# Attention with a relative position bias, then a mixture of adapters: a planner that knows of a shared port, bias multiplies over two chunks, and a reordered opening

## The chip, the core and the metric

The kernel runs on one core of one Trainium2 chip. Its time is the device time of one execution, in microseconds. Before the change it is 222.62 us, the median of 3 runs (222.09 to 223.76). One further execution was taken by the hardware profiler; all rows of a profile shown here come from such single executions.

In the profile PE is the TensorE matmul, PEld its weight load, DVE is VectorE, ACT is ScalarE, POOL is GpSimd and SP is SyncE; a "q" behind a name (SPq, ACTq) is the engine's queue issuing a DMA. L65 is the line of a helper through which all VectorE and GpSimd instructions pass, so these are told apart by the names of what they write and read.

## The reference, cut to what matters

Two stages follow each other. The first is attention over 8 batches, 8 heads, 576 positions and 64 columns a head, with a bias that depends on the distance of two positions alone:

```python
scores = scale * np.matmul(q, k.transpose(0, 1, 3, 2))
n = np.abs(pos[:, None] - pos[None, :])
bucket = np.where(n < half, n, np.minimum(large, n_buckets - 1))
scores = scores + bias_table[bucket].transpose(2, 0, 1)[None]
attn = softmax(scores); x = attn @ v
```

All distances from 128 on share one bucket. Since softmax does not change when one number is taken off a whole row, the bias can be taken relative to that last bucket; it then differs from zero only in a band around the diagonal.

The second stage treats the 4608 rows of x (512 columns). Eight gates are computed by `x @ w_gate`, the two largest are kept and turned into weights, and each chosen adapter adds `weight * (x @ A[e]) @ B[e]` to x, with A and B of rank 16.

## The kernel before

The unit of work is a *pair*: two heads of one batch. There are 32 pairs, four to a batch, taken in order. Of the 576 positions, 512 form the main part (four key chunks of 128 keys, each against 512 queries and both heads) and 64 form the tail. Pair i passes through these steps:

- SyncE issues the loads: k in two transfers (L164), q in one (L170), v in two (L164); once a batch the tails of k and q (L176, four transfers) and of v (L182, two).
- GpSimd casts k, q and v to bfloat16 (kb, qb, vn), and once a batch the tails (tl, vt).
- PE transposes kb and qb into a PSUM tile (kqps, L264), and VectorE copies it to SBUF (kqT).
- PE computes the scores: chunks 0 to 3 are the main part (L281), each a PSUM tile of 128 x 1024. Chunk 4 (L286 to L294) holds the tail keys and the tail queries; there the bias is added by matmuls against MT and MH. ScalarE takes the exp of each chunk (L301, p<-sc), five a pair. One small exp a batch (ptt) covers tail against tail.
- VectorE multiplies the band of chunks 0 to 3 by the exp of the bias (`band`, L304; p<-p,M), one instruction a chunk. A middle chunk has 768 elements a partition, an outer one 512.
- PE multiplies with v (L324 to L333, pv), VectorE takes the reciprocal of the sums (rc) and scales (x<-pv,rc).

After the fourth pair of a batch follows the *mixture* of that batch (L631), interleaved with the next batch's pairs: transposes of x (xps, VectorE copies xT), products with A and the gates (zp, zf), a gate chain of small instructions on GpSimd, VectorE and ScalarE, one more transpose (zT), the product with B and the addition of x on VectorE (o<-sc,x), and the store. The last batch has a version of its own, `final` (L802), after the last pair.

The bias tables are made at the start (`bias_prep`, L510). The bias table is loaded, its last row taken off, and spread over distances into g_sb (8 x 512) by fifteen or so small copies. ScalarE takes the exp of the 512 columns into one half of gg, and VectorE scales the other half. gg is written to memory (g_d) and read back with one element's shift a partition: Mr for the first two heads and MHr by GpSimd's queue, MTr and the rest of Mr by SyncE's. VectorE reverses these into M (the band's factors), MT, MH and MHT.

The order of all this is not written by hand. Every step is entered with an engine, a cost, its dependences and a due time (`add`, L97). A list scheduler then places the steps one by one: for each engine it works out when each ready step could start (`start_of`, L985), takes of those that can start at once the one with the earliest due time, and over the engines the earliest. It knows of three rings of buffers, which are given out in turn: three PSUM tiles for scores ("sc"), two for everything else ("ms"), three output tiles ("o"). Instructions are emitted in the planned order, so each engine's queue is fixed, and the waits between engines follow from the data.

One rule concerns GpSimd. From pair 9 on, the casts of k, q and v carry a mark (`win`): such a cast is delayed by PATIENCE (1500 ns in the plan) unless VectorE has just been given an instruction that reads PSUM. Then it is placed right after, and made to wait for the VectorE instruction before that one by an added dependence:

```python
if o.ps and lastv is not None and free["PL"] <= t + 120:
    ws = [c for c in cand["PL"] if c.win and start_of(c) <= t + 120]
```

Of the kernel before, what the change touches and what calls it, by code (L numbers as in the profile page):

```python
# [27 lines left out]
def kernel(  # L28
# [51 lines left out]
    scp = ctx.enter_context(tc.tile_pool(name="sc_ps", bufs=3, space=PSUM))  # L80
    msp = ctx.enter_context(tc.tile_pool(name="misc_ps", bufs=2, space=PSUM))


    class Op:
        __slots__ = ("eng", "cost", "lat", "fn", "deps", "due", "ring", "end", "done",
                     "users", "left", "ready", "n", "dma", "ps", "win", "after", "inst", "follow")
# [3 lines left out]
    PATIENCE = 1500  # L90
    TA = 6
    OD = 5.0
    LAT = {"PE": 190, "ACT": 190, "DVE": 110, "PL": 200, "SP": 5000}
    ops = []
    rings = {"ms": [2, []], "o": [3, []], "sc": [3, []]}

    def add(eng, cost, fn, deps=(), due=0.0, lat=None, ring=None, nb=0.0, dma=None, ps=False):  # L97
        o = Op()
        o.ps, o.win, o.after, o.inst, o.follow = ps, False, None, None, None
# [8 lines left out]
    def mm(n):  # L108
        return 16 + n * 0.417 if n <= 130 else 4 + n * 0.417

    def dv(n, fast):
        return 60 + n / (1.92 if fast else 0.96)
# [15 lines left out]
    g_sb = cp.tile([H, 512], FP32, tag="g_sb")  # L128
    bsub = cp.tile([H, NB], FP32, tag="bsub")
    gg = cp.tile([H, 2, 512], BF16, tag="gg")  # L130
    ge, gl = gg[:, 0, :], gg[:, 1, :]
# [34 lines left out]

    def q_dma(i, eng):
        b, hp = divmod(i, HP)
        stg[(i, "qf")] = ldp.tile([128, 2, 256], FP32, name="qf", tag="qf")
        EN[eng].dma_start(out=stg[(i, "qf")], in_=q[b, 2 * hp:2 * hp + 2, 0:S4, :]  # L170
                          .rearrange("h (p j) d -> p h (j d)", j=4))
# [13 lines left out]
    def load(i):  # L185
# [5 lines left out]
        R["lk", i] = [add("SP", 480, lambda h=h: nat_dma(i, h, "kf", k), pre[:1], dk + .01 * h,  # L191
                          nb=nk, dma=580) for h in range(2)]
        eq = "SP" if i else "ACT"
        R["lq", i] = [add(eq, 480, lambda: q_dma(i, eq), pre[1:2], dk + .02 if i else -75, nb=nk, dma=730)]
        R["lv", i] = [add("SP", 480, lambda h=h: nat_dma(i, h, "vf", v), pre[2:], dv_ + .01 * h,
                          nb=nv, dma=580) for h in range(2)]

    def loadt(b, due):
        n = 0.0 if b == 0 else 14000.0 if b == 1 else 6500 + 1030 * due
        for w in range(2):  # L200
            for e in range(2):
                en = "SP"
                R["lt", b, w, e] = add(en, 550, lambda w=w, e=e, en=en: tail_dma(b, w, e, en), [g_("ct", b - 2)],
                                       due + .01 * e, nb=n, dma=290)
        for e in range(2):
            R["lvt", b, e] = add("SP", 550, lambda e=e: vtail_dma(b, e), [g_("cvt", b - 2)],
                                 due + (4 if b == 0 else 3) + .01 * e,
                                 nb=8000.0 if b == 0 else n + 3000, dma=290)

    def ck_(i, e):  # L210
        kq[(i, 0)] = ntp.tile([128, 4, 2, D], BF16, name="kb", tag="kb")
        bcopy(EN[e], kq[(i, 0)], stg.pop((i, "kf")))

# [52 lines left out]
    def T_ev(i, w=None):  # L266
        if not w:
            kqT[i] = kqp.tile([128, 2, S4], BF16, name="kqT", tag="kqT")
        if w is None:
            DVE.tensor_copy(kqT[i], st[(i, "kqps")])  # L270
        else:
            DVE.tensor_copy(kqT[i][:, w], st[(i, "kqps")][:, w])
# [26 lines left out]
    def softmax_exp(i, c):  # L299
        p = pp.tile([128, 1024], BF16, name=f"p{c}", tag=f"p{c}")  # L300
        AC.activation(p, st.pop((i, c, "sc")), ACT.Exp, scale=scale)  # L301
        probs[(i, c)] = p

    def band(i, g):  # L304
        b, hp = divmod(i, HP)
        p = probs[(i, g)]
        q0, q1 = max(0, 32 * (g - 1)), min(128, 32 * (g + 2))
        x0 = q0 - 32 * (g - 1)
        pm = p.rearrange("p (h j q) -> p h j q", h=2, j=4)[:, :, :, q0:q1]
        DVE.tensor_tensor(pm, pm, M[:, 2 * hp:2 * hp + 2, :, x0:x0 + q1 - q0],  # L310
                          op=ALU.mult)

    def pv(i, part, h):
        b, hp = divmod(i, HP)
        vn, vt = vnb[i], vts[b % 2]
        if part == 0:
# [4 lines left out]
        if part < 4:  # L321
            for s in range(4):
                o = h * 512 + s * 128
                PE.matmul(acc[:, s, :], lhsT=p[:, o:o + 128], rhs=vn[:, part, h, :],  # L324
                          start=(part == 0 and s == 0), stop=False, skip_group_check=True)
# [32 lines left out]
    def mx_ev(b, half):  # L358
        if half == 0:
# [24 lines left out]
    def gate_chain(b, w, nt, pre, due):  # L384
# [42 lines left out]
        pd = d if ge_ == "DVE" else 160  # L427
        if w == "L":
            pre = [add("DVE", d, lg, pre, due)]
        ms = [add("DVE", 70, lambda t=t: mx(t), pre, due + .01) for t in range(nt)]  # L430
# [655 lines left out]
```

## Time and profile before

| what | us |
|---|---|
| median of the runs | 222.62 |
| the profiled execution, own time | 223.12 |
| its span, first to last instruction | 221.3 |
| PE busy | 181.6 (82%) |
| VectorE busy | 182.6 (82%) |
| ScalarE busy | 163.8 (74%) |
| GpSimd busy | 108.9 (49%) |
| mean share of the 16 DMA engines, by the queue table | 70% on q1 |
| first exp starts | 8.26 |
| last exp ends | 201.65 |

The busy times are unions of records; records on one engine may overlap a little where the pipeline does. A group's row gives the busy time, the mean of one instruction in ns, and after the second bar the idle time of the engine just before such instructions, with what ended it. A row of stretches gives, for each engine, the busy time in that stretch and the number of instructions, then the granted TensorE clock, the DMA share and GB/s. A row of the timeline gives the start, the length, the engine, the line and what is written and read.

### The profile page before, as it was taken

The numbers are of one execution on the slowest core, as the hardware profiler recorded it, in microseconds if no ns is written. First come the engines' busy times: TensorE is split into PE (matmuls) and PEld (weight loads), VectorE is DVE, ScalarE is ACT, GpSimd is POOL, SyncE is SP. The second block draws the span as 40 slices with busy tenths as digits, with TensorE's granted clock in tenths as the row PEclk, the third lists the DMA queues.
The fourth block names the chain that finished last, engine by engine and source line by source line (L and its number), as shares of the span: only waits on it lengthen the run. The fifth ranks groups of instructions, "written<-read, shape, count | busy, mean of one in ns | idle before, by whom it ended". The sixth has DMA issues, their size and how long they took to land.

```text
span 221.3 us, 7356 instructions
## 1 busy us (share of the span) xinstructions
PE 181.6 (82%) x2895; PEld 124.7 (56%) x2895; DVE 182.6 (82%) x475; ACT 163.8 (74%) x189; POOL 108.9 (49%) x216
## 2 busy tenths in 40 slices
PE   6616882998998897999998889899899988989570
PEld 6304561576665575676666656666466755758330
DVE  4437973489999899999999889999999999898652
ACT  3526895488787897998879598998897987984121
POOL 6674654565754545545545455576572654040000
PEclk9985999599999999999999999999999999999858
DMA  5799789989969989887879789989992004003306
GB/s 137 172 229 190 184 144 206 210 192 200 236 164 268 283 176 224 262 211 175 208 187 308 181 193 291 264 187 243 266 280 62 3 0 192 1 6 115 123 5 232
DMA packets 99706, 39.90 MB, mean 180 GB/s; under 512 B 87648, under 2 KB 96640, under 8 KB 99672
## 3 DMA queue, kind: packets, MB, share of 16 engines
q1 hardware_dynamic: 98960, 38.76, 70.2%
q8 instruction: 22, 0.36, 0.7%
q0 software_dynamic: 160, 0.39, 0.6%
q10 hardware_dynamic: 552, 0.28, 0.4%
q14 instruction: 12, 0.10, 0.1%
HBM read 29.97 MB, written 9.45 MB: 178 GB/s over the span
## 4 chain that ended last, share of the span: by engine, by line
DVE 37%; PE 31%; SPq 12%; DMA 11%; issue 3%; POOL 3%; ACT 2%; POOLq 0%; ACTq 0%; DVEq 0%
DVE p L65 11%; PE pv L324 8%; SPq L164 7%; PE sc L281 6%; DVE x L65 6%; DVE o L65 5%; DVE kqT L65 4%; DMA vf<-in_v_dram 3%; PE kqps L264 3%; DMA kf<-in_k_dram 3%; DVE xT L65 2%; SPq L170 2%; PE pv L333 2%; PE zp L444 2%; DVE rc L65 2%
## 5 line engine op out<-in xcount | busy, mean ns | idle before, releaser
L301 ACT ACTIVATE p<-sc 128x1024 bf16<-128x1024 f32 x160 | 153.7, 1025 | 31.3 <-PE sc L281 22.3
L65 DVE TENSOR_TENSOR p<-p,M 128x512 bf16<-128x512 bf16 (+1 forms) x128 | 68.1, 542 | 0.4
L324 PEld LDWEIGHTS <-p 128*128 128x128 bf16 x1024 | 39.1, 99 | 21.0 <-issue 14.3
L324 PE MATMUL pv<-vn,p 128*128 128x65 bf16 x1024 | 45.7, 196 | 6.0 <-DVE kqT L65 2.8
L281 PE MATMUL sc<-kqT 64*128 64x512 bf16 x256 | 40.6, 392 | 2.1 <-ACT p L301 0.9
L65 DVE TENSOR_TENSOR x<-pv,rc 128x320 bf16<-128x320 f32 (+1 forms) x65 | 31.2, 481 | 1.1
L65 POOL CAST vn<-vf 128x512 bf16<-128x512 f32 x32 | 21.1, 660 | 20.5 <-DVE p L65 11.0
L65 POOL CAST kb<-kf 128x512 bf16<-128x512 f32 x31 | 20.4, 658 | 19.9 <-DMA kf<-in_k_dram 10.9
L65 DVE COPY kqT<-kqps 128x1024 bf16<-128x1024 bf16 (+1 forms) x33 | 21.9, 667 | 9.6 <-PE kqps L264 9.4
L65 POOL CAST qb<-qf 128x512 bf16<-128x512 f32 x31 | 20.3, 656 | 6.2 <-DMA qf<-in_q_dram 1.3
L328 PE MATMUL pv<-vn,p 128*128 128x65 bf16 x256 | 18.5, 195 | 0.0
L333 PE MATMUL pv<-vt,p 128*128 128x65 bf16 x256 | 18.5, 195 | 0.0
L264 PE MATMUL kqps<-ident,kb 128*128 128x128 bf16 x128 | 12.7, 222 | 6.6 <-POOL kb L65 4.0
L65 POOL CAST tl<-tf 64x512 bf16<-64x512 f32 x16 | 10.5, 656 | 14.2 <-DMA tf<-in_q_dram 13.8
L65 DVE TENSOR_TENSOR o<-sc,x 128x1024 f32<-128x1024 f32 x14 | 17.0, 1215 | 0.4 <-PE sc L474 0.3
L65 DVE RECIPROCAL rc<-pv 128x5 f32<-128x5 f32 x64 | 12.0, 188 | 5.9 <-PE pv L333 5.5
L264 PEld LDWEIGHTS <-kb 128*128 128x128 bf16 x128 | 8.0, 98 | 14.5 <-POOL kb L65 4.9
L281 PEld LDWEIGHTS <-kqT 64*128 64x128 bf16 x256 | 7.9, 95 | 11.1 <-issue 5.1
L286 PE MATMUL sc<-tlT,kqT 128*128 128x128 bf16 x128 | 12.5, 221 | 1.6 <-ACT p L301 1.2
L264 PE MATMUL kqps<-ident,qb 128*128 128x128 bf16 x128 | 12.7, 222 | 1.1 <-POOL qb L65 1.1
L333 PEld LDWEIGHTS <-p 128*128 128x128 bf16 x256 | 12.4, 99 | 1.0 <-issue 0.8
L328 PEld LDWEIGHTS <-p 128*128 128x128 bf16 x256 | 12.4, 99 | 0.5 <-issue 0.5
(119 smaller groups left out, 281.5 us busy)
## 6 DMA issues: line engine op xcount, KB each, us to landing
kf<-in_k_dram SPq DMA_DIRECT2D x64, 128.0 KB, 3.5
vf<-in_v_dram SPq DMA_DIRECT2D x64, 128.0 KB, 3.5
qf<-in_q_dram SPq DMA_DIRECT2D x31, 256.0 KB, 3.9
out_dram<-o SPq DMA_DIRECT2D x14, 512.0 KB, 3.7
tf<-in_k_dram SPq DMA_DIRECT2D x16, 64.0 KB, 3.8
tf<-in_q_dram SPq DMA_DIRECT2D x16, 64.0 KB, 3.4
vtf<-in_v_dram SPq DMA_DIRECT2D x16, 64.0 KB, 3.1
out_dram<-ol SPq DMA_DIRECT2D x4, 256.0 KB, 2.6
```

Of the source, the lines that this page charges most:

```text
L65: self.inst = f(*a, **k)
L164: SY.dma_start(out=stg[(i, key)][:, :, h, :], in_=src[b, 2 * hp + h, 0:S4, :].rearrange("(g p) d -> p g d", p=128))
L170: EN[eng].dma_start(out=stg[(i, "qf")], in_=q[b, 2 * hp:2 * hp + 2, 0:S4, :] .rearrange("h (p j) d -> p h (j d)", j=4))
L264: PE.transpose(ps[:, w, j * 128:(j + 1) * 128], t[:, j], ident)
L281: PE.matmul(sc[:, h * 512:(h + 1) * 512], lhsT=t[s, 0, c * 128:(c + 1) * 128], rhs=t[s, 1, :], start=True, stop=True)
L286: PE.matmul(sc[:, g * 128:(g + 1) * 128], lhsT=t[:, 0, g * 128:(g + 1) * 128], rhs=tt[:, 1, hp, :], start=(g == 0), stop=True, skip_group_ ...
L301: AC.activation(p, st.pop((i, c, "sc")), ACT.Exp, scale=scale)
L324: PE.matmul(acc[:, s, :], lhsT=p[:, o:o + 128], rhs=vn[:, part, h, :], start=(part == 0 and s == 0), stop=False, skip_group_check=True)
L328: PE.matmul(acc[:, 4, :], lhsT=p[:, g * 128:(g + 1) * 128], rhs=vn[:, g, h, :], start=False, stop=False, skip_group_check=True)
L333: PE.matmul(acc[:, s, :], lhsT=l, rhs=vt[:, hp, h * D1:(h + 1) * D1], start=False, stop=True, skip_group_check=True)
L444: PE.matmul(st[(b, w, "zp", t0)][:, t - t0, :], lhsT=xT[:, c, t * 128:(t + 1) * 128], rhs=AW[:, c, :], start=(t == t0 and c == 0), stop=(c ...
```

## The change

It has several parts.

*The planner.* Bias multiplies are marked (`sb`). In the plan, such a multiply does not start before GpSimd is free, and a GpSimd instruction does not start before the last marked multiply has ended, nor where a ready one would soon start. On the chip, every GpSimd instruction but a DMA gets a dependence on a VectorE instruction: on the last one placed if that is marked, else on the one before it (`tie`). The old marks `win`, `ps` and PATIENCE are gone. A table OFF adds an offset to the due time of each kind of step; its values were found by a search outside the kernel. Costs and latencies in the plan are new. PSUM tiles are given out by name: the planner takes the slot that comes free first, instead of the next in turn.

*The multiplies.* The four main chunks of a pair lie in one tile of 4 x 1024. One instruction multiplies the two middle chunks (1536 elements a partition), one the two outer ones (1024).

*Pair 0 and the bias tables.* k of pair 0 comes in three transfers; its first 128 positions are cast and transposed by themselves. ScalarE casts k and VectorE casts q (before the other way round). The exp is taken of the 32 table columns before they are spread, not of the 512 after; the spreading writes both halves of gg at once. All five reads of g_d are issued by SyncE.

*Order.* The exps run in the order chunks 0 to 3 of pair 0, chunks 0 to 3 of pair 1, chunk 4 of pair 0, chunk 4 of pair 1, and then pair by pair as before. The products with v take part 1, 2, 0, 3, 4, 5, and the last pair's first two parts need only the middle multiply.

```diff
-    def band(i, g):
-        b, hp = divmod(i, HP)
-        p = probs[(i, g)]
...
-        DVE.tensor_tensor(pm, pm, M[:, 2 * hp:2 * hp + 2, :, x0:x0 + q1 - q0],
-                          op=ALU.mult)
+    def band(i, mid):
+        hp = i % HP
+        t = probs[i]
+        m = M[:, 2 * hp, 0, (0 if mid else 32):]
+        if mid:
+            n, pd, md = 96, [[1024 + 32, 2], [128, 8]], [[0, 2], [96, 8]]
+            p0 = t[:, 1, 0:1]
+        else:
+            n, pd, md = 64, [[3 * 1024 + 64, 2], [128, 8]], [[-32, 2], [96, 8]]
+            p0 = t[:, 0, 0:1]
...
+        DVE.tensor_tensor(pm, pm, ma, op=ALU.mult)
```

```diff
+        if o.sb:
+            t = max(t, free["PL"])
+        elif o.eng == "PL" and not o.dma:
+            t = max(t, sb_free[0])
...
+                for c in cand["DVE"]:
+                    if c.sb:
+                        r_ = max(c.ready, free["DVE"])
+                        if r_ < t + o.cost - YIELD and r_ + c.cost > t:
+                            t, again = r_ + c.cost, True
+            a = tie()
+            if a is not None:
+                t = max(t, a.end)
         return t
+    def tie():
+        return lastv[1] if lastv[1] is None or lastv[1].sb else lastv[0]
...
+        if o.eng == "PL" and not o.dma:
+            o.after = tie()
         place(t, o)
         if o.eng == "DVE":
-            if o.ps and lastv is not None and free["PL"] <= t + 120:
-                ws = [c for c in cand["PL"] if c.win and start_of(c) <= t + 120]
...
-            lastv = o
+            lastv[:] = lastv[1], o
```

```diff
+        due = due + OFF.get(key, 0.0)
...
-        z = add("DVE", 400, lambda: DVE.memset(g_sb, 0.0), (), -45.0)
-        s = add("DVE", 90, sub, [l], -20)
+        s = add("DVE", 180, sub, [l], -60)
+        x = add("ACT", 200, lambda: AC.activation(b2[:, 0, :], bsub, ACT.Exp), [s], -60)
...
-        e = add("ACT", 500, lambda: AC.activation(ge, g_sb, ACT.Exp), rs, -40)
...
-        m0 = [add("PL", 300, lambda: mr(PL, 0, 2), [d], -60, dma=700)]
+        m0 = [add("SP", 450, lambda: mr(SY, 0, 2), [d], -60, dma=640)]
+        h_ = [add("SP", 450, lambda e=e: mhr(e), [d], -48, dma=350) for e in range(2)]
...
-        e = ("DVE", "ACT") if i == 0 else ("PL", "PL")
+        e = ("ACT", "DVE") if i == 0 else ("PL", "PL")
...
+    seq = [(i, c) for i in range(2) for c in range(4)] + [(0, 4), (1, 4)]
+    seq += [(i, c) for i in range(2, NPAIR) for c in range(5)]
```

## The prediction

> **What bounds the kernel now.** I read the busy row of the page first, then a table of three stretches cut at exps that I can count, then the groups by form, the waits, and the timelines of ScalarE and SyncE in the opening.
>
> ```profile
> PE 181.6 (82%) x2895; PEld 124.7 (56%) x2895; DVE 182.6 (82%) x475; ACT 163.8 (74%) x189; POOL 108.9 (49%) x216
> ```
>
> ```profile
> core 0: us, PE busy (x) PEld busy (x) DVE busy (x) ACT busy (x) POOL busy (x), PEclk, DMA share, GB/s
> 8.26:46.88 38.62, 25.35 (x351) 16.08 (x349) 22.70 (x51) 24.95 (x27) 21.26 (x36) 0.82 0.93 188
> 46.88:196.70 149.82, 136.20 (x2293) 94.72 (x2292) 141.15 (x362) 129.06 (x147) 80.77 (x153) 1.00 0.74 191
> 196.70:221.30 24.60, 14.75 (x196) 9.39 (x194) 14.49 (x44) 7.20 (x13) 1.43 (x3) 0.82 0.32 107
> ```
>
> The middle row holds pairs 5 to 30 (26 pairs, 130 exps): 5.76 us a pair, of which VectorE is busy 5.43, ScalarE 4.96, GpSimd 3.11. VectorE has 0.33 us a pair free, so it sets the pace. PE's 5.24 is no rival of equal weight, since its records overlap (a 65-column matmul is recorded at 196 ns, and sixteen of them pass in 0.66). The first row is limited otherwise: 25 exps in 38.62 us at a DMA share of 0.93. The last exp ends at 201.65; 19.65 us of tail follow.
>
> ```profile
> L65 DVE TENSOR_TENSOR p<-p,M 128x768 bf16<-128x768 bf16 x64 | 39.9, 626 | 0.0
> L65 DVE TENSOR_TENSOR p<-p,M 128x512 bf16<-128x512 bf16 x64 | 29.2, 457 | 0.3
> L65 DVE COPY kqT<-kqps 128x1024 bf16<-128x1024 bf16 x31 | 21.2, 684 | 9.2 <-PE kqps L264 9.0
> L65 POOL CAST kb<-kf 128x512 bf16<-128x512 f32 x31 | 20.4, 658 | 19.9 <-DMA kf<-in_k_dram 10.9 <-DVE p L65 2.8 <-PE kqps L264 2.7
> ```
>
> The bias multiply ("band") is VectorE's largest item: 69.1 us. Its means hide two values. Sorted by what GpSimd does meanwhile, a 768 band takes 544 ns alone (27 of 64) and 684 where GpSimd is busy for over 60% of it (22); a 512 band 409 (23) and 524 (24); a cast 0.61 alone, 0.71 to 0.76 beside a band. The kqT copy takes 686 and 682, so it doesn't care. [...]
>
> ```profile
> 0.75 0.61 ACTq L538 DMA_DIRECT2D btT<-in_bias_table_dram  x1
> 1.38 0.41 ACTq L170 DMA_DIRECT2D qf<-in_q_dram  x1
> 5.36 0.60 ACT L153 CAST qb<-qf 128x512 bf16<-128x512 f32 x1
> 6.13 0.32 ACTq L548 DMA_DIRECT2D g_d<-gg  x1
> 8.26 1.94 ACT L301 ACTIVATE p<-sc 128x1024 bf16<-128x1024 f32 x2 [2.30 <-PE sc L281]
> 10.56 1.94 ACT L301 ACTIVATE p<-sc 128x1024 bf16<-128x1024 f32 x2 [0.36 <-PE sc L281]
> 18.65 1.02 ACT L301 ACTIVATE p<-sc 128x1024 bf16<-128x1024 f32 x1 [6.15 <-PE sc L294]
> 22.65 4.69 ACT L301 ACTIVATE p<-sc 128x1024 bf16<-128x1024 f32 x5 [0.65 <-PE sc L281]
> 40.64 1.94 ACT L301 ACTIVATE p<-sc 128x1024 bf16<-128x1024 f32 x2 [4.41 <-PE sc L281]
> ```
>
> Here ScalarE stands 6.15 us: chunk 4 of pair 0 needs MT and MH, which come back from memory by way of g_d. Five exps in a row take 4.69, 0.92 apart. Pair 2 starts at 25.4, pair 4 at 40.64 after another 4.41 us.
>
> **The change part by part.**
>
> Bands, four to two a pair. Elements stay the same (2560). What falls away is two fixed costs. In the records 512 elements take 409 ns and 768 take 544, a slope of 0.53 ns an element and 138 ns fixed. In a backlog the next record starts before this one ends: a band alone adds 462 and 336 ns of busy time, about 65 fixed. [...] VectorE is backlogged here, so the spacing decides: 0.13.
>
> Collisions. In the middle stretch a band adds 545 and 382 ns on average against 462 and 336 alone: 2 x (83 + 46) = 0.26 us a pair. The new plan lets a GpSimd instruction start only behind the last band, and counts GpSimd's end before a band. The chip holds only the first half: GpSimd waits for a VectorE instruction, no band waits for GpSimd. [...] I go by the rows: gain 0.26 if all vanish, 0 if the casts slip, below nothing only by the starving in the second rival. I take 0.21 with a rest of collisions, and 0.04 for the small two-operand mk<-zf (283 against 97 ns, seven).
>
> VectorE's need is then 5.43 - 0.13 - 0.21 - 0.04 = 5.05 us a pair. ScalarE's is 4.96 and is next: five exps at 0.92, ptt (0.60 in four pairs) and its starts. GpSimd's is 3.0 (94 of its casts fall from 0.66 to 0.61), but it may no longer use the 1.47 us of bands: 4.5 of 5.05. Three queues in fixed order, each nearly full, don't reach 100%; before, VectorE reached 94%. With 97% I take 5.2 us a pair (bounds 4.97, ScalarE without a gap, and 5.76, nothing won).
>
> The added wait. 147 of GpSimd's 204 helper instructions carry a VectorE wait, before 74 of 205. Behind a waiting one stand the casts of the next pair; then the transposes on PE, the kqT copy, the scores, and the exp. The plan casts about six chunks ahead of use, so a wait of one VectorE instruction (0.5) is covered; without this cover it would come whole, 0.5 a pair.
>
> Opening. q of pair 0 moves ahead of the bias table on ScalarE's queue (0.6 earlier), its cast to VectorE (0.43 for 0.60), k comes in three transfers, scores follow chunk by chunk. But the q cast now stands in front of the bias subtraction, which ran at 3.32 and will run near 5.2; with the exp of 32 columns and thirteen fills (0.095 each), g_d goes out near 7.4 for 6.13. The copy of kqT stands among these fills, so the first exp is no earlier: 8.2. g_d takes 2.90 to land: 10.3.
>
> ```profile
> 9.04 0.37 SPq L561 DMA_DIRECT2D MTr<-g_d  x1
> 9.46 0.60 SPq L182 DMA_DIRECT2D vtf<-in_v_dram  x1
> 10.10 0.60 SPq L551 DMA_DIRECT2D Mr<-g_d  x1
> 10.75 1.68 SPq L164 DMA_DIRECT2D kf<-in_k_dram  x2
> ```
>
> All five bias reads now stand in SyncE's queue (three came by GpSimd's, issued 9.68 to 11.8). SyncE is through its loads at about 9.0 and waits 1.3 us for g_d with pair 2's k and everything after it behind that wait; reads at 10.3 to 13.1, k of pair 2 at 13.1 for 10.75. MH and MT are copied near 15.5 for 18.2. ScalarE meanwhile has the eight exps of chunks 0 to 3 of pairs 0 and 1 (7.4 us, to 15.6), then chunk 4 of both and ptt from 16.5 to 19. Pair 2's k lands near 17.5; two casts, transposes, copy and scores (3.2) give its first exp at 21, where it was 25.4. Gain 4.4.
>
> Weights: the four A_f transfers (4.28 on SyncE) now stand behind k and q of pair 4, so the 4.41 at 40.64 should shrink; I count that inside the 5.2.
>
> Tail. The two output additions of batch 6 (1.22 each) stood ahead of the last pair's x and xT on VectorE; now the first stands behind xT, the second in the gate chain. One of them, 1.2, leaves the path: 18.4 for 19.65.
>
> Buffers by name instead of by turn, and the key offsets, cost no instruction; the order they make is in the 5.2. If it is bad, pairs wait as in the first row (38.62 us for five pairs, 7.7 each).
>
> Sum: 21 + 30 x 5.2 + 18.4 = 195.4 us of span. The profiled execution had 223.12 for a span of 221.3, 1.8 around it, and lies 0.5 above the median of 222.62. So 197.2, I say **197 us**, 0.885 of before.
>
> **The rivals.**
>
> *Ideal.* ScalarE never waits after pair 2 at 5.0 a pair and pair 2 starts at 19: 19 + 150 + 18 + 1.8 = 189. For it: 39 exps in the 40 us from 140 to 180 already now. Against: the waits on scores (22.3 us in the whole run) come from several causes. 7 in 100.
>
> *Collisions stay.* Casts run late, meet the bands, only merging and opening pay: 5.43 - 0.13 - 0.04 = 5.26 at 95% is 5.54; 21 + 166 + 18.4 + 1.8 = 207, up to 214 with nothing won in the middle. For it: bands do not wait. 14 in 100.
>
> *GpSimd starves the pairs (slower).* One queue takes casts for k, q, v and the tails, in order.
>
> ```profile
> POOL vn L65 <- DVE p L65: 11.0, 7, 3.8
> ```
>
> Already now seven v casts stand 11.0 us behind bands, up to 3.8. If each of some six GpSimd instructions a pair loses 0.1 to its wake and the two windows between bands lose half a cast each (0.6), its need is 4.5 + 0.6 + 0.6 = 5.7, and one such 3.8 us wait in every second pair makes 6.3 on average with the tail reads: 21 + 190 + 19 + 1.8 = 232. It decides from 6.1 a pair on ((222.6 - 1.8 - 39.4)/30 = 6.05). Against it: six chunks of lead and three buffers for kb and qb. 9 in 100.
>
> *It doesn't do what it says* (plan and chip differ so that order gains nothing): within 1%, 220 to 225, with the opening's gain eaten in the middle. 3 in 100.
>
> **How the numbers follow.** The forecast has 67 in 100, with its own range 190 to 204. For eight in ten I reach down to 189 and up to 212, so the ideal case and most of the collision case are inside. About 1% is what a measurement of this kernel tells from no change. Faster 0.88, same 0.03, slower 0.09.
>
> **What would show it.** Bands: 64 of 1536 and 64 of 1024 elements near 0.94 and 0.68 us alone; collisions show as a long upper tail. Opening: eight exps without a 6.15 us gap, first exp near 8.2, pair 2 near 21. Middle: ScalarE at 93% or more, VectorE's busy time near 160 us in all. Starving: long GpSimd waits on VectorE rows, followed by PE on kb and qb and ScalarE on scores. I'm wrong if ScalarE's gaps in the middle don't shrink, whatever the bands take.

## The result, and the profile after

The changed kernel takes 213.32 us (210.36 to 216.7), 0.950 of before (95% interval 0.939 to 0.961): faster, but 16 us above the forecast of 197 and just outside its range (to 212). Medians are of all executions, while ratios leave out those that are over 1.5% slower than the fastest of their kernel, so the two differ a little. On another chip it later took 214.00 us, 0.957 (0.951 to 0.963). Each experiment below is set against executions of before on the same chip (medians 224.2 to 225.4). The profiled execution shown here had 212.76 for a span of 211.0.

The busy row of the page, after:

```profile
PE 180.1 (85%) x2895; PEld 128.2 (61%) x2895; DVE 172.7 (82%) x413; ACT 161.8 (77%) x190; POOL 98.7 (47%) x213
```

The table of stretches, cut at the first exps of pairs 0, 2 and 8 (exp 0, 10 and 40) and of pair 31 (exp 155):

```profile
core 0: us, PE busy (x) PEld busy (x) DVE busy (x) ACT busy (x) POOL busy (x), PEclk, DMA share, GB/s
9.06:24.80 15.74, 10.56 (x107) 6.83 (x106) 8.37 (x17) 9.98 (x11) 6.27 (x13) 0.67 0.78 176
24.80:62.27 37.47, 31.16 (x489) 22.28 (x487) 25.14 (x55) 29.13 (x33) 17.90 (x32) 0.86 0.90 196
62.27:187.00 124.73, 117.65 (x2015) 83.64 (x2014) 118.28 (x269) 112.68 (x131) 67.08 (x138) 1.00 0.80 205
187.00:211.00 24.00, 15.01 (x240) 10.54 (x236) 16.88 (x54) 7.47 (x14) 2.13 (x6) 0.98 0.32 110
```

The third row holds 23 pairs (8 to 30): 5.42 us each. Cut in the same way, before has 5.72, with VectorE busy 94.2% of the stretch. After, VectorE is busy 118.28/124.73 = 94.8%, 5.14 us a pair where it was 5.39. On the face of it VectorE sets the pace as before, at a lower need; but PE's records fill 117.65/124.73 = 94.3% of the same row, and the experiments will show that the reading is only half of it. The second row, six pairs at a DMA share of 0.90 and a granted clock of 0.86, takes 6.25 us a pair.

The groups by form, VectorE and then GpSimd:

```profile
L65 DVE TENSOR_TENSOR p<-p,M 128x1536 bf16<-128x1536 bf16 x32 | 31.5, 983 | 0.9 <-ACT p L375 0.2
L65 DVE TENSOR_TENSOR p<-p,M 128x1024 bf16<-128x1024 bf16 x32 | 22.7, 708 | 1.0
L65 DVE COPY kqT<-kqps 128x1024 bf16<-128x1024 bf16 x31 | 21.3, 686 | 12.3 <-PE kqps L336 12.3
```

```profile
L65 POOL CAST kb<-kf 128x512 bf16<-128x512 f32 x31 | 19.0, 613 | 26.0 <-DVE p L65 10.8 <-DMA kf<-in_k_dram 4.4 <-DVE o L65 3.4
```

The multiplies take 54.1 us for 69.1; alone, a record is 949 and 685 ns. Of 128 multiplies 73 were overlapped by GpSimd for over a quarter of their length, now 10 of 64 are. The casts of k and q are at 613 and 617 ns on average, where one alone took 0.61 us, so these hardly collide any more; those of v are at 661 as before (660), two of them at 1.07 and 1.38 us. But the casts now wait for VectorE, which the last column shows.

The opening, ScalarE's timeline and then SyncE's:

```profile
8.71 0.30 ACTq L630 DMA_DIRECT2D g_d<-gg  x1
9.06 7.44 ACT L375 ACTIVATE p<-sc 128x1024 bf16<-128x1024 f32 x8 [3.07 <-DMA kf<-in_k_dram]
16.34 0.65 ACT L328 ACTIVATE ptt<-ttps 128x512 bf16<-128x512 f32 x1
19.04 2.09 ACT L375 ACTIVATE p<-sc 128x1024 bf16<-128x1024 f32 x2 [2.05 <-PE sc L362]
24.80 1.94 ACT L375 ACTIVATE p<-sc 128x1024 bf16<-128x1024 f32 x2 [3.67 <-PE sc L349]
27.90 1.94 ACT L375 ACTIVATE p<-sc 128x1024 bf16<-128x1024 f32 x2 [1.15 <-PE sc L349]
```

```profile
12.24 0.60 SPq L643 DMA_DIRECT2D MTr<-g_d  x1
12.88 0.58 SPq L633 DMA_DIRECT2D Mr<-g_d  x1
13.51 3.05 SPq L205 DMA_DIRECT2D kf<-in_k_dram  x2
```

The eight exps run without a gap as forecast, but g_d goes out at 8.71, MT is copied at 17.86, and pair 2 starts at 24.80, hardly earlier than the 25.4 of before.

So the span of 211.0 stands against 195.4 forecast, and the miss of 15.6 splits so:

| part | forecast | measured | miss |
|---|---|---|---|
| first exp of pair 2 | 21.0 | 24.80 | 3.8 |
| pairs 2 to 7 (to 62.27) | 6 x 5.2 | 37.47 | 6.3 |
| pairs 8 to 31 (to the last exp's end, 191.98) | 24 x 5.2 | 129.71 | 4.9 |
| tail | 18.4 | 19.02 | 0.6 |

The second profile of the changed kernel has the same span, 211.1, and splits it otherwise: pair 2 at 24.42, pairs 2 to 7 in 35.67, the rest to the last exp's end in 132.0. So a part moves by some 2 us from one execution to the next.

### The profile page after: what moved, and what is told of

Its sections match the earlier page's. It is cut to its first block, busy times and chain, and to the rows that moved or that the text cites. A ratio compares the mean times of both kernels' runs of the same rounds, so it can differ in the third digit from the quotient of the medians.

```text
span 211.0 us, 7252 instructions
## 1 busy us (share of the span) xinstructions
PE 180.1 (85%) x2895; PEld 128.2 (61%) x2895; DVE 172.7 (82%) x413; ACT 161.8 (77%) x190; POOL 98.7 (47%) x213
## 4 chain that ended last, share of the span: by engine, by line
DVE 42%; PE 21%; SPq 16%; DMA 7%; issue 5%; ACT 4%; POOL 1%; DVEq 0%; POOLq 0%; ACTq 0%
DVE p L65 15%; SPq L205 7%; DVE x L65 6%; DVE o L65 6%; DMA kf<-in_k_dram 5%; PE kqps L336 5%; PE sc L349 4%; ACT p L375 3%; SPq L225 3%; DVE kqT L65 3%; PE pv L402 3%; DVE zf L65 3%; DVE rc L65 3%; PE zp L522 3%; SPq L664 2%
## 5 line engine op out<-in xcount | busy, mean ns | idle before, releaser
L65 DVE TENSOR_TENSOR p<-p,M 128x1536 bf16<-128x1536 bf16 (+1 forms) x64 | 54.1, 846 | 1.9 <-ACT p L375 0.2
L402 PEld LDWEIGHTS <-p 128*128 128x128 bf16 x1024 | 38.8, 100 | 21.9 <-issue 7.8
L65 DVE COPY kqT<-kqps 128x1024 bf16<-128x1024 bf16 (+3 forms) x34 | 22.2, 654 | 12.5 <-PE kqps L336 12.3
L65 POOL CAST kb<-kf 128x512 bf16<-128x512 f32 x31 | 19.0, 613 | 26.0 <-DVE p L65 10.8
L65 POOL CAST qb<-qf 128x512 bf16<-128x512 f32 x31 | 19.0, 616 | 14.2 <-DVE zf L65 3.6
L349 PEld LDWEIGHTS <-kqT 64*128 64x128 bf16 x256 | 8.4, 95 | 12.6 <-issue 5.6
L354 PE MATMUL sc<-tlT,kqT 128*128 128x128 bf16 x128 | 13.1, 228 | 0.0
L360 PE MATMUL sc<-kqT,tlT 128*128 128x512 bf16 x32 | 12.9, 403 | 0.0
L411 PE MATMUL pv<-vt,ptt 128*128 128x65 bf16 x64 | 12.5, 195 | 0.0
L406 PEld LDWEIGHTS <-p 128*128 128x128 bf16 x256 | 12.5, 100 | 0.0
```

The lines of the kernel that those rows point to most:

```text
L65: self.inst = f(*a, **k)
L349: PE.matmul(sc[:, h * 512:(h + 1) * 512], lhsT=t[s, 0, c * 128:(c + 1) * 128], rhs=t[s, 1, :], start=True, stop=True)
L354: PE.matmul(sc[:, g * 128:(g + 1) * 128], lhsT=t[:, 0, g * 128:(g + 1) * 128], rhs=tt[:, 1, hp, :], start=(g == 0), stop=True, skip_group_ ...
L360: PE.matmul(sc[:, 512:1024], lhsT=tt[:, 0, hp, :], rhs=t[:, 1, :], start=True, stop=False, skip_group_check=True)
L406: PE.matmul(acc[:, 4, :], lhsT=p[:, g * 128:(g + 1) * 128], rhs=vn[:, g, h, :], start=False, stop=False, skip_group_check=True)
L411: PE.matmul(acc[:, s, :], lhsT=l, rhs=vt[:, hp, h * D1:(h + 1) * D1], start=False, stop=True, skip_group_check=True)
```

## The experiments

Theory: the gain comes from a lower need of VectorE (merged multiplies, no collisions), and the miss from its fill (the share of the time in which it is busy), from the opening and from late transfers. Rivals: the added waits cost more than the collisions they avoid; the order that the offsets make carries the gain; VectorE isn't what sets the pace at all. In all tables "pace" is (exp 155 - exp 40)/23 of the profiled execution, and so is the busy time a pair.

This pace is a mean of 23 pairs, and in some profiles one or two of them spoil it: the granted TensorE clock is 0.5 in stretches of 3.4, 6.8 or 10.2 us, and where one lies in the middle, the pair there takes 1.2 to 5.4 us longer. So "pace at full clock" is given beside it: the mean of those of the 23 pairs that no such stretch touches or has touched in the pair before.

### What each part carries

**Without the added waits** (same planned order):

```diff
-        if o.after is not None:
+        if False and o.after is not None:
             tc.add_manual_dep(PL.inst.ins, ...
```

> The changed kernel with the same planned order, but without the added dependences of GpSimd on VectorE. If the collisions were what the change took away in the middle (pace 5.76 to about 5.4 us a pair), they come back: multiplies of 1536 and 1024 elements grow from 0.95 and 0.69 by 0.1 to 0.2 us on average in the half that meets a cast, VectorE needs 0.15 to 0.25 us a pair more, and the time is 217 to 221 us. Rival, that the waits hold GpSimd's queue and cost more than the collisions: 205 to 210 us.

216.28 us, 0.964 (0.955 to 0.972). VectorE's need is 5.32 a pair for 5.14, collisions are back (42 of 64 multiplies):

```profile
L65 DVE TENSOR_TENSOR p<-p,M 128x1536 bf16<-128x1536 bf16 x32 | 34.5, 1079 | 0.6
L65 DVE TENSOR_TENSOR p<-p,M 128x1024 bf16<-128x1024 bf16 x32 | 24.7, 771 | 1.0
```

Leaving the waits off is not faster, and the collisions that they take away are worth 0.18 us a pair of VectorE's time by these two profiles (0.16 against the second one). In the end this is 2 to 3 us, a little less than expected, and the interval overlaps those of the changed kernel.

**The merged multiplies alone, in the kernel before**, with the planner of before:

```diff
-                n_ = 2 * 4 * (96 if c in (1, 2) else 64)
-                R["bd", i, c] = add("DVE", dv(n_, True), lambda i=i, c=c: band(i, c),
-                                    [x, R["M", hp]], t0 + c + 1.8)
...
+        R["bd", i, 0] = add("DVE", dv(1536, True), lambda i=i: band(i, True),
+                            [R["ex", i, 2], R["M", hp]], t0 + 2 + 1.8)
+        R["bd", i, 3] = add("DVE", dv(1024, True), lambda i=i: band(i, False),
+                            [R["ex", i, 3], R["bd", i, 0]], t0 + 3 + 1.8)
```

> The kernel before with one part of the change alone: two multiplies a pair over two chunks each, in place of four. By spacing, two instructions fewer save 0.13 us a pair or 4 us in all: 218 to 220 us. If the fixed part of a record (138 ns) counted whole: 9 us, 213 to 215. [...]

230.99 us, 1.030 (1.022 to 1.038): slower than before, where a saving of 4 or of 9 us was put down. VectorE's need fell by 0.27 to 5.12, twice what merging was to give, since fewer multiplies now meet GpSimd (35 of 64, for 73 of 128). But VectorE's fill fell from 0.942 to 0.867, and the pace rose to 5.91. Whether the later start of the first multiply (it waits for the exp of chunk 2) or the order that this plan makes costs the fill isn't separated. The stretch of pairs 8 to 30, with the columns of the table above:

```profile
67.84:203.76 135.92, 117.52 (x2001) 83.04 (x2020) 117.81 (x272) 113.57 (x129) 72.45 (x130) 1.00 0.69 181
```

**The offsets left out** (`OFF = {}`), all else as changed:

> The changed kernel with the table of offsets empty, so that the plan follows its own due times. If the searched priorities matter on the chip, VectorE's share of busy time in the middle falls below 94% and the time is 216 to 224 us. If the chip does not follow the plan closely enough for them to matter: 211 to 215 us.

228.57 us, 1.019 (1.011 to 1.027): slower than before too, and beyond both branches. The same stretch:

```profile
62.18:200.59 138.41, 120.15 (x1995) 86.29 (x2017) 121.93 (x272) 112.60 (x131) 64.75 (x135) 0.98 0.71 186
```

Exp 40 comes at 62.2 as in the changed kernel; the loss lies behind it, 6.02 us a pair (5.89 at full clock) at a fill of 0.881. The offsets, which add no instruction, are worth some 15 us in this kernel. No run gave the kernel before such a table, so what a search would have brought there is not known.

**The merged multiplies cut in two again**, in the changed kernel, the order and the waits kept:

```diff
-        DVE.tensor_tensor(pm, pm, ma, op=ALU.mult)
+        for x in range(2):
+            pc = bass.AP(tensor=pm.tensor, offset=pm.offset + x * pd[0][0], ap=[pm.ap[0]] + pd[1:] + [[1, n]])
+            mc = bass.AP(tensor=ma.tensor, offset=ma.offset + x * md[0][0], ap=[ma.ap[0]] + md[1:] + [[1, n]])
+            DVE.tensor_tensor(pc, pc, mc, op=ALU.mult)
```

> The changed kernel with its order, offsets and waits exactly as they are, but each merged multiply issued as two instructions of one chunk each, back to back (chunks 1 and 2, then 0 and 3). It prices the merging alone. By the spacing of the records (65 ns fixed) two more instructions cost 0.13 us a pair, 32 x 0.13 = 4 us: 216 to 218. By the 138 ns fixed in each record it is 0.28 a pair, 9 us: 221 to 223. If VectorE does not set the pace after the change, nothing: 212 to 214.

214.12 us, 0.956 (0.950 to 0.962), against 0.950 and 0.957 for the merged form. VectorE's need rose to 5.30, by 0.13 to 0.15, and the time hardly moved: the third branch. The pace did move, to 5.58, at full clock to 5.50 from 5.42 and 5.45: less than half of what the need rose by. So VectorE is on the path, but not alone, and the next runs ask what else there is.

**Two tiles for the four chunks**, so that the outer multiply no longer waits for the middle one:

```diff
-            t = pp.tile([128, 4, 1024], BF16, name="p", tag="p")
+            tm = pp.tile([128, 2, 1024], BF16, name="pm", tag="pm")
+            to = pp.tile([128, 2, 1024], BF16, name="po", tag="po")
```

> The changed kernel with two tiles a pair, one for the two middle chunks and one for the two outer ones, so that the second multiply no longer waits for the end of the first. If this wait is why the multiplies add 0.90 and 0.65 us alone where 0.87 and 0.60 were reckoned, VectorE gains up to 0.08 us a pair: 210.5 to 212.5. If not, 213 as the changed kernel.

212.95 us, 0.949 (0.940 to 0.958): nothing that these intervals could show, and the pace at full clock is 5.42.

### What sets the middle

Here work is left out of the changed kernel, with its order kept.

**Without the outer multiply:**

```diff
-        DVE.tensor_tensor(pm, pm, ma, op=ALU.mult)
+        if mid:
+            DVE.tensor_tensor(pm, pm, ma, op=ALU.mult)
```

> The changed kernel without its second multiply (chunks 0 and 3 stay without the bias, so these probabilities are not the reference's): 0.65 to 0.69 us of VectorE's work a pair fall away, all else and the order stay. If VectorE sets the pace of 5.4 us in the middle, VectorE's need falls to 4.5, ScalarE is next with 4.9 busy and its gaps, about 5.15 a pair, and pairs 8 to 31 gain 24 x 0.27 = 6.5 us: 205 to 208. If waits in a fixed order set it, with no engine full, less than a third of that comes: 211 to 213. More than 8 us would say that VectorE's share of the gaps is larger than I think.

210.80 us, 0.941 (0.936 to 0.946), near the second branch. Half a microsecond a pair of VectorE's work is gone, and the pace is 5.47. VectorE was not the only bound. GpSimd's waits, between 62 and 180 us, changed their cause; the columns are the total, the number and the longest, in us. First the changed kernel, then this run:

```profile
POOL kb L65 <- DMA kf<-in_k_dram: 0.8, 1, 0.8
```

```profile
POOL kb L65 <- DMA kf<-in_k_dram: 15.2, 10, 3.6
```

That made the transfers the suspect.

**Without the 512 KB stores**, by themselves and together with the outer multiply:

```diff
-        SY.dma_start(out=out[b * S:b * S + S4, :].rearrange("(p j) c -> p j c", j=4)[:, t:t + 2],
-                     in_=st.pop((b, t // 2, "o")))
+        st.pop((b, t // 2, "o"))
```

> The changed kernel without the fourteen 512 KB stores of the finished rows (those rows of the output stay unwritten): 7.2 of about 40 MB of transfers fall away, no engine's computation changes. With the multiply of chunks 0 and 3 left out, the pace stayed at 5.47 us a pair though VectorE fell from 5.14 to 4.64 busy, and GpSimd's waits for landing k grew from 1.1 to 16.3 us. If VectorE sets the changed kernel's pace and the loads stand just behind it, taking transfers alone gives little: 209 to 212. If the loads alone set it: 200 to 204. If some fixed order of the queues sets it with neither: 211 to 213.

> Both taken at once: no 512 KB stores (those rows unwritten) and no multiply of chunks 0 and 3 (these probabilities without their bias). If VectorE and the loads are two limits of nearly the same height, only both together free the pace, to ScalarE's 4.9 busy and its gaps, 5.05 to 5.15 a pair: 199 to 203 by pairs 2 to 31. If the fixed order or PE sets 5.4: 209 to 212, as with one of them.

**Without the outer multiply and with fewer products**, to ask for PE:

```diff
-        if part < 4:
+        if part in (0, 3):
+            pass
+        elif part < 4:
```

> No multiply of chunks 0 and 3 and none of the products of chunks 0 and 3 with v (so these keys are missing from the output): VectorE falls by 0.5 us and PE by sixteen matmuls of 65 columns, some 0.65 us, a pair; the transfers stay. If the loads set the pace once VectorE is relieved: as without the multiply alone, 209 to 212 and about 5.45 a pair. If PE (5.0 to 5.1 busy of 5.45) was the second limit: 5.1 a pair, 200 to 204.

| left out | us | ratio (interval) | pace | pace at full clock | VectorE busy | PE busy |
|---|---|---|---|---|---|---|
| nothing | 213.32 | 0.950 (0.939 to 0.961) | 5.42 | 5.42 | 5.14 | 5.12 |
| nothing, other chip | 214.00 | 0.957 (0.951 to 0.963) | 5.52 | 5.45 | 5.17 | 5.10 |
| outer multiply | 210.80 | 0.941 (0.936 to 0.946) | 5.47 | 5.47 | 4.64 | 5.02 |
| stores | 210.85 | 0.940 (0.933 to 0.947) | 5.44 | 5.38 | 5.11 | 5.16 |
| both | 205.77 | 0.920 (0.915 to 0.926) | 5.21 | 5.21 | 4.57 | 5.05 |
| outer multiply, two products | 208.41 | 0.932 (0.926 to 0.938) | 5.44 | 5.30 | 4.57 | 4.84 |

Each of the two alone takes some 2.5 us off the time and leaves the pace about where it was; only both together free it, and the time falls by 7.5 us, to a point between the two branches of that run. The single pairs show how. Without the stores, pairs 10 to 18 take the time that they take in the changed kernel, to 0.01 us (pair 13, say, 5.71 both times): transfers do not set these pairs, the engines in their fixed order do. Without the outer multiply most pairs get shorter, and a few much longer. Pair 21 takes 7.16 us, where the changed kernel has 5.71 and the run with both left out 5.47. The cast of k of pair 23 waits for its load there; an instruction of the mixture's gate chain (zt) stands behind it in GpSimd's queue, and PE stands until that one is done:

```profile
132.08 0.61 POOL L65 CAST kb<-kf 128x512 bf16<-128x512 f32 x1 [2.34 <-DMA kf<-in_k_dram]
132.66 0.40 POOL L65 TENSOR_TENSOR zt<-zf,gate 128x128 bf16<-128x128 f32 x1
133.11 0.23 PE L545 MATMUL ztps<-ident,zt 128*128 128x128 bf16 x1 [1.61 <-POOL zt L65]
```

So the half microsecond of VectorE is worth some 0.2 us a pair where the loads are in time, and where it is left out, late loads take the gain back in single pairs.

The run with fewer products doesn't clear PE. Its stretch has a granted clock of 0.97; at full clock the pace is 5.30, and the fastest of pairs 8 to 29 takes 4.52 us, where it is 4.81 in the five rows above it. PE's busy time fell by only 0.2, not by the 0.65 that was to be taken off, and loads are late here too. So PE holds some pairs, and whether it holds the mean isn't settled.

The stretch with both left out shows what stands next: PE's records fill 116.26/119.75 = 97% of it, ScalarE's 112.06/119.75 = 94%. Which of the two limits there was not tested:

```profile
60.45:180.20 119.75, 116.26 (x2015) 84.00 (x2014) 105.16 (x244) 112.06 (x130) 67.29 (x137) 1.00 0.70 163
```

**Bytes or time of issue?** Two runs move the loads of pairs 9 to 31 forward by 3 us in the planned order, without the outer multiply and complete:

```diff
-    for t, n, o in sorted(order, key=lambda x: x[:2]):
+    tk = {id(o): t for t, n, o in order}
+    for i in range(9, NPAIR):
+        for o in R["lk", i] + R["lq", i] + R["lv", i]:
+            tk[id(o)] -= 3000
+    for t, n, o in sorted(order, key=lambda x: (tk[id(x[2])], x[1])):
```

> As the run without the multiply of chunks 0 and 3 (210.80, 5.47 us a pair), with k, q and v of pairs 9 to 31 standing 3 us earlier in the sync engine's order, ahead of the stores and tail loads that stood before them; bytes as before. If the time of issue limits the loads: as without the stores, 5.2 a pair, 204 to 207, and GpSimd's waits on k (16.3 us there) gone. If bytes limit them: 209 to 212 with those waits unchanged.

212.46 us, 0.942 (0.932 to 0.952): the time did not fall. By the row of waits, k is now in time (this profiled execution took 213.24, within its runs of 209.98 to 213.97):

```profile
POOL kb L65 <- DMA kf<-in_k_dram: 0.6, 1, 0.6
```

But such a row books a wait to the releaser that came last, and the longest waits for loads are booked elsewhere. The second half of pair 13's k was issued at 74.03 and landed at 80.22. Its cast started right then and is booked to PE; behind it stood the gate chain's sum (sm), behind that VectorE, and behind that PE, for 3.08 us. Meanwhile, at 82.2, the granted clock was halved for 6.8 us (the last row, one of stretches):

```profile
80.37 0.61 POOL L65 CAST kb<-kf 128x512 bf16<-128x512 f32 x1 [3.85 <-PE sc L349]
81.50 0.20 POOL L65 TENSOR_TENSOR sm<-ex 128x4 f32<-128x4 f32 x1
81.73 0.18 DVE L65 RECIPROCAL sm<-sm 128x4 f32<-128x4 f32 x1 [3.25 <-POOL sm L65]
83.44 0.64 PE L523 MATMUL zp<-AW,xTt 128*128 128x136 bf16 x4 [3.08 <-DVE x L65]
82.20:89.00 6.80, 5.26 (x38) 3.78 (x40) 5.12 (x13) 2.15 (x3) 3.15 (x9) 0.50 0.81 188
```

Pair 12 took 10.68 us for it, and pair 28, in a like place, 8.28. The 19 pairs away from half clock average 5.19, as with both left out; that leaves out the late pairs themselves. Counted by the landing times, casts waited 22.8 us for loads in the middle without the outer multiply, 11.2 here, and 11.2 and 17.3 in the two profiles of the changed kernel. So this profile shows fewer late loads, and the first branch's pace between them, while the run's time shows no gain; its other executions have no profile, so what held them stays open. The test that remained was to keep each store in its place and queue, with an eighth of its bytes:

```diff
+        SY.dma_start(out=out[b * S:b * S + S4, :].rearrange("(p j) c -> p j c", j=4)[0:16, t:t + 2], in_=o_[0:16])
```

> Without the multiply of chunks 0 and 3, and each of the fourteen stores in its place but with 16 of its 128 partitions (the other rows stay unwritten): 64 KB for 512. If the bytes of the stores are what held the pace: as without the stores, 205 to 207 and 5.2 us a pair. If it is their places in the queue or the output buffers that wait for them: as with whole stores, 210 to 212 and 5.45 a pair. Between, if both.

205.78 us, 0.919 (0.911 to 0.926), pace 5.23: the same as without stores. So it is their bytes and not their places in the queue. The wait by which they reach the pace in the profiles above is that of a cast for a late load, with the gate chain behind it.

The complete kernel with the loads earlier, and then both on one chip in five rounds:

> The changed kernel complete, with the loads of pairs 9 to 31 standing 3 us earlier in the sync engine's order. VectorE still holds 5.4 a pair if it is one of the two limits: 210 to 213. If the late loads were part of VectorE's 5 per cent of gaps: 207 to 210. If the stores, now later, hold the output buffers that the additions wait for: above 214.

> The changed kernel itself, beside the next run on one chip: 211 to 214, exp 40 at 60 to 62.

> The changed kernel complete, with k, q and v of pairs 9 to 31 standing 3 us earlier in the sync engine's order. If earlier loads close some of VectorE's gaps: 1 to 2 us below the changed kernel on the same chip. If VectorE or the bytes hold the pace: within 0.5 us of it.

211.04 us, 0.942 (0.934 to 0.950); then 212.38 against 214.00 for the changed kernel, 0.947 (0.940 to 0.954) against 0.957 (0.951 to 0.963). It is about 1% lower both times, at the edge of what these intervals tell apart. It is the fastest complete kernel found here, by little. The pace at full clock is 5.42 and 5.36: with VectorE's work whole, loads in time change the middle little.

### The opening and pairs 2 to 7

**One adapter of eight loaded:**

```diff
-                out=A_f[:, c], in_=moe_A[:, c * 128:(c + 1) * 128, :]
+                out=A_f[:, c, 0:1], in_=moe_A[0:1, c * 128:(c + 1) * 128, :]
```

> The changed kernel, but each of the four A transfers brings one adapter of eight and the rest of A is zero, so the adapters' product is not the reference's; the order is the same. If the loads set the pace up to 60 us, the 4.3 us that SyncE spends on A (27.9 to 32.2) come free, the gaps of ScalarE at 52.2 and 55.6 (5.0 us together) mostly vanish, and the time is 208 to 210 us (3 to 5 less). Rival, that VectorE or PE sets that stretch: within 1 us of the changed kernel.

211.72 us, 0.943 (0.933 to 0.954): 1.6 us below the first measurement of the changed kernel, within the spread; exp 40 at 60.0. (The rest of A is set to zero by one more GpSimd instruction.) Since the changed kernel itself had exp 40 at 60.1 in its other profile, even that doesn't stand as a gain.

**v of three pairs not loaded** (3, 5 and 7 use that of the pair before), 768 KB less in this stretch:

```diff
+        if key == "vf" and i in (3, 5, 7):
+            return
+        if key == "vf" and i in (2, 4, 6):
+            stg[(i + 1, key)] = stg[(i, key)]
```

> The changed kernel, but v of pairs 3, 5 and 7 isn't loaded; these pairs use the v of the pair before (their rows of the output are not the reference's). 768 KB fall away before exp 40, at the 197 GB/s of that stretch 3.9 us. If pairs 2 to 7 wait for the bytes of their loads: exp 40 at 56 to 58 (60 to 62 in the runs so far), and the end 3 to 4 us earlier, 208 to 210. If the order of the opening or TensorE's lower clock there (0.86) sets these pairs: exp 40 at 60 to 62, 211 to 214.

208.92 us, 0.931 (0.923 to 0.940), 4.4 us lower; in the profiled execution (210.57, the slowest of its four) exp 40 comes at 57.5, where four profiles of the complete kernel, with the loads of pairs 9 to 31 in either place, have it between 59.2 and 62.3. That is the first branch: these pairs wait for bytes. The rival, TensorE's lower clock, is at most the smaller part: the second profile of the changed kernel had the full clock here (first row) and still took 35.67 us for 37.47, and this run, at 0.95, took 32.79:

```profile
24.42:60.09 35.67, 27.45 (x483) 19.59 (x487) 25.38 (x54) 28.72 (x32) 20.05 (x32) 1.00 0.88 194
24.73:57.52 32.79, 28.36 (x483) 20.46 (x487) 26.33 (x54) 29.09 (x32) 17.44 (x31) 0.95 0.88 197
```

**k of pair 2 issued ahead of the bias reads**, first in the emitted order alone, then in the plan, with the bias copies due later:

```diff
+    for o in R["lk", 2]:
+        tk[id(o)] = tk[id(R["m0"][0])] - 1
```

```diff
-        nk = (0, 3000, 8500, 11000, 13000)[i] if i < 5 else 6500 + 1030 * (t0 - 12)
+        nk = (0, 3000, 0, 11000, 13000)[i] if i < 5 else 6500 + 1030 * (t0 - 12)
...
-        dk, dv_ = (-50 + .1 * i if i < 2 else t0 - 14), (-45 if i == 0 else t0 - 8)
+        dk, dv_ = (-50 + .1 * i if i < 2 else -61 if i == 2 else t0 - 14), (-45 if i == 0 else t0 - 8)
...
-                [m1] if hp else m0, 5 * hp + (1 if hp else -20))
+                [m1] if hp else m0, 5 * hp + (5 if hp else -20))
```

> The changed kernel with the two k transfers of pair 2 issued ahead of the reads of g_d on SyncE, in the 0.7 us in which it waits. If pair 2 starts late because these transfers land at 20.3 and 22.2 behind the reads of the bias, they land near 14, and pair 2's first exp moves from 24.8 to 21 to 22; the bias reads land 0.5 to 1 us later. As the whole supply is short, less than that remains at the end: 211 to 213 us. If ScalarE's start of pair 2 hangs on something else: 24.8 stays.

> The changed kernel planned with k of pair 2 loaded at the very start, ahead of the bias reads, and the bias copies of heads 2 to 7 due four chunks later, so that pair 2's casts, transposes and copy stand ahead of the waits for the bias in every queue; the planner orders the rest anew with the same offsets. Pair 2's first exp should come near 20 to 21 in place of 24.8. If the opening's miss of 3.8 us is lost for good: 208 to 210. If loads in pairs 2 to 7 are what limits, the gain is given back there by exp 40: 211 to 214. If the new order of the rest is bad for the offsets searched for the old one: above 214, with a lower fill of VectorE in the middle.

213.56 us, 0.950 (0.941 to 0.959), and 215.15 us, 0.962 (0.956 to 0.968): no gain from the first, whose pair 2 started at 26.28, and the second is if anything a little slower. In the first, k of pair 2 landed by 13.5, but its cast is the next instruction of GpSimd and waited 6.22 us for VectorE, which stood at the bias copies:

```profile
14.82 0.61 POOL L65 CAST qb<-qf 128x512 bf16<-128x512 f32 x1
21.64 0.88 POOL L65 CAST kb<-kf 128x512 bf16<-128x512 f32 x1 [6.22 <-DVE M L65]
```

In the second the casts of pairs 1 and 2 were done by 10.5, and pair 2 still started at 24.62. VectorE's timeline there:

```profile
19.18 0.29 DVE L65 COPY MT<-MTr 128x512 bf16<-128x512 bf16 x1 [1.85 <-DMA MTr<-g_d]
19.39 1.68 DVE L65 TENSOR_TENSOR p<-p,M 128x1024 bf16<-128x1024 bf16 x2
22.62 1.03 DVE L65 COPY M<-Mr 128x768 bf16<-128x768 bf16 x2 [1.55 <-DMA Mr<-g_d]
```

VectorE stands until MTr has landed, the multiplies of pairs 0 and 1 stand behind that copy, PE waits for them (21.13) with pair 0's products, and pair 2's scores stand behind those (24.0). The changed kernel has the same order of events, MT at 17.86, the multiplies at 18.07 and pair 2 at 24.80; there k of pair 2 also lands late, its second half at 22.18, so two chains end near each other, and taking one away gains nothing. No run took the bias reads out, so this is read from the timelines and not shown by a test.

## Why the prediction was right or wrong

**The direction and the sizes of the VectorE instructions: right.** 0.94 and 0.68 us were forecast, 949 and 685 ns came. Merging was put at 0.13 us a pair of need by the spacing of records (two of about 65 ns) and not at 0.28 by the 138 ns fixed in each record: cutting them again costs 0.13 to 0.15, by which of the two profiles of the changed kernel it is set against. Collisions were put at 0.21: taking the waits off brings back 0.16 to 0.18. That the two engines share a port, as the title has it, no run shows: the profile before shows only the longer time, 684 ns on average where GpSimd was busy for over 60% of a 768 multiply and 544 without it. How a single collision ends they don't show either (worst record: 979 ns).

**The added wait: covered in the middle, as said; not in the opening.** GpSimd's waits on VectorE rose from 34 to 73 us in all, and yet leaving the added ones off was not faster (216.28 us), so the starving rival fell. In the opening the 6.22 us above show one such wait with no lead ahead of it, once the data is early.

**"The A_f stall is inside the 5.2": wrong, and the largest part of the miss, 6.3 us.** The 5.2 was taken for all pairs from pair 2 on, and nothing was put for transfers in pairs 2 to 7, which took 6.25 each (5.95 in the second profile, at full clock). The stretch before, at a DMA share of 0.93 and 7.7 us a pair, was in view, and I gave its slowness to order alone ("if it is bad"). These pairs wait for the bytes of their loads: 768 KB less gave 2.9 us against one profile and 4.7 against the other. The adapters' own bytes gave nothing clear.

**"With 97% I take 5.2 us a pair": wrong by 4.9 us in pairs 8 to 31.** VectorE's need came down to 5.14 where 5.05 was forecast, and the fill stayed at 94.8%; the pace to the end of the last exp was 5.40. The 97% was put between 100% and the 94% of before, without a reason of its own. This fill is no property of VectorE's queue: with less VectorE work it sinks (0.849 without the outer multiply) while the pace stays.

**"ScalarE's is 4.96 and is next": not borne out.** With VectorE's need half a microsecond lower, late loads take back what it brings; with those gone too the pace is 5.2, PE's records fill 97% of it and ScalarE's 94%. I had set PE aside because its records overlap, and the runs don't decide between the two. A count of bytes does not find the limit either: the 188 GB/s at a share of 0.93 in the first row before, by my estimate some 202 GB/s if full, and 1.10 MB a pair (loads, tails and stores by the table of DMA issues) make 5.4 us, the measured pace, but by luck, since the middle after moves 205 GB/s at a share of 0.80, and the pace without the stores is the same (5.44).

**The opening: direction right, size off.** First exp 9.06 for 8.2, g_d issued 8.71 for 7.4, MT copied 17.86 for 15.5, pair 2 24.80 for 21. I put pair 2 behind its own k alone; MTr took 5.6 us to land and holds pairs 0 and 1, whose products stand ahead of pair 2's scores. An earlier k gained nothing.

**"Buffers by name and the key offsets cost no instruction; the order they make is in the 5.2": no instruction, but the part without which no gain is left.** Without the offsets the kernel is 1.9% slower than before, and merging alone, in the old plan, 3.0% slower. I had this only as a mishap ("7.7 each") and gave "it doesn't do what it says" 3 in 100; I gave the order no term of its own.

**Tail:** 19.02 for 18.4; a gain of 0.6 for the forecast 1.2.

**The signs.** ScalarE is busy for 90% of the middle where 93% or more was to show; its gaps did shrink, from 0.76 to 0.52 us a pair. VectorE's busy time is 172.7 us, not near 160; but that figure doesn't follow from the prediction's own sum, since 182.6 less 32 x 0.38 is 170.4.

The rival nearest to the time was "collisions stay" (207, up to 214), for a reason that did not hold: they nearly vanished.

## What to carry to other kernels

An engine that is busy 95% of the time is a candidate for the bound and not more: leave some of its work out and see whether the pace moves (here it went from 5.42 to 5.47 us a pair, with 0.5 us of VectorE's work gone). If it doesn't, the gain may have been taken back by something else, so try reliefs in pairs. Compare single units of work and not their mean alone: where a unit takes the same time with some of the transfers left out (pair 13 here, 5.71 us both times), the engines' order sets it, and where a few are long, follow the queue that stands there back to a late load, by the landing time and not by the name that a row of waits gives. In this kernel with its planned queues the cheaper instruction alone was a loss (1.030 of before), and the order was worth more than it (the offsets, some 15 us); price the two apart.

## What the runs showed of the hardware

*A stretch at half clock in the middle came after a short stand of PE.* In the middle of the twenty profiles (pairs 8 to 30) the granted clock fell to 0.5 ten times, for 3.4 or 6.8 us, and each time PE had stood for 0.9 to 3.1 us, beginning 0.9 to 3.3 us earlier. About twice as many such stands were followed by none. In the runs with the changed kernel's order the pair there took 1.2 to 5.4 us longer, the stand itself included.

*Transfers of one size took very different times to land.* MTr, 128 KB, took 5.6 us from issue in the changed kernel and 4.2 before; the two loads of k of the same size issued behind the bias reads took 6.8 and 7.5 us in the changed kernel, where the median of such a load is 3.5. Whether MTr's short rows (64 bfloat16) add to it isn't shown.
